# Turning h earlier among the transposes of a fused attention and mixture-of-experts kernel

## The chip, the core and the metric

The kernel runs as one program on one core of a Trainium2 chip. The metric is the device time of one execution in microseconds (us). Three executions of the kernel before took 520.6, 523.1 and 522.89 us, so its median is 522.89 us. The execution that the profiler recorded is a separate one; it took 523.23 us.

A core has five engines with an instruction queue each, and each queue runs in order. TensorE (PE in the profile) multiplies matrices and transposes; PEld is its loading of stationary operands, which overlaps the multiplications. VectorE is DVE, ScalarE is ACT, GpSimd is POOL, SyncE is SP and mostly issues DMA transfers. Engines wait for each other through semaphores.

## The reference

Sigmoid attention over 8 batches, 12 heads, 448 positions and 64 dimensions gives 3584 rows (tokens) of 768 values. Each row that passes a skip test then goes through one of eight experts, and the expert's result, weighted by a gate, is added to the row:

```python
scores = scale * np.matmul(q, k.transpose(0, 1, 3, 2)) - np.log(S)
attn = 1.0 / (1.0 + np.exp(-scores))
x = np.matmul(attn, v)            # then as rows of 12 * 64 = 768 values
do_compute = (x @ w_skip) > 0
xc = x[do_compute]
logits = xc @ w_gate
e_idx = np.argmax(logits, axis=1)
# gate_w: the softmax weight of the chosen expert
for e in range(8):
    mask = e_idx == e
    h = np.maximum(xc[mask] @ w1[e], 0.0)           # 768 -> 1024
    y[mask] = gate_w[mask, None] * (h @ w2[e])      # 1024 -> 768
out = x.copy()
out[do_compute] = xc + y
```

The change touches only the expert part: `xc @ w1`, the ReLU, and `h @ w2`.

## The kernel before, in words

**Attention** comes first, in 48 steps of two heads each, until about 285 us of the profiled span. It also sorts the tokens by expert into a list in DRAM. Two blocks of 128 tokens of the fullest expert follow, written out one by one (`b0`, `b1`), until about 324 us.

**The loop.** The other tokens go through a loop of 14 rounds, from 324.6 us to the end. Each round takes one block of tokens of one expert and branches on its kind:

- a full block of 128 tokens, `block(i, last)`. Its weights are there as two parts, `wh` (rounded to the type fp32r) and `wl` (what the rounding left), and so is its input, `xh` and `xl`. A product is the sum of three: high by high, high by low, low by high. With `last` true the block also splits the raw weights of the next expert (`hi1`, `hi2` on ScalarE, `lo1`, `lo2` on VectorE).
- a 64-token block, `half(i)`, in plain fp32 from the raw weights.
- a 32-token block, `few(i)`, likewise in plain fp32.

In this run the order of kinds is: full, half, full, half, then full and few in turn five times. That makes seven full blocks, two half blocks and five few blocks. The first and the sixth full block are those with `last` true.

**Order of the work.** The body of each kind stands in a manual schedule: every engine runs its instructions in the order in which the code issues them, and the framework adds only the semaphores. What is written earlier is queued earlier on its engine.

**A full block.** `gemm1(h, ...)` makes one half (512 columns) of h with 18 matmuls of 512 columns into the PSUM bank `ph[h]`. `relu(h)` on ScalarE moves it to `hs` in SBUF. `turn_h(h)` transposes it with four transposes of 128x128 into `pht[h]`. `split_h(h)` makes `hh[h]` on ScalarE and `hl[h]` on VectorE. `gemm2(j)` (six matmuls of 384 columns) uses one of eight 128-column pieces of h: pieces 0 to 3 come from the first half, 4 to 7 from the second. In between, the rows of the next block, `xn`, are transposed by `turn_x` (three transposes for each of two halves, into `pxt`); `fetch` then lets GpSimd gather the rows of the block after that into `xn`; `ready_x` copies `pxt` to `xh` and `xf` on ScalarE and subtracts to `xl` on VectorE. At the end `weigh_sum` scales the result on VectorE, and `put` adds it to the output by an indirect DMA on GpSimd. In a plain full block `put` holds a `drain` of GpSimd before it looks at the result.

**A half block.** `side` makes h with 24 matmuls, two of which share the PE array: the two halves of h lie on partitions 0 to 63 and 64 to 127 of one bank, `ph[0]`. The ReLU goes to `hs`, four transposes of h go to `pht[0]` (pieces 0 and 1) and `ph[1]` (pieces 2 and 3), ScalarE copies them to `ht`, and 32 matmuls make the result in `py[1]`. `take_rec`, two small copies, is VectorE's first work of the block.

**What stands in the queues around the change.** In the half block VectorE runs, in order: `take_rec`, the two subtractions of `ready_x`, the two scalings of `weigh_sum` and the copies of `advance`. A `last` block ends with these lines, which put five subtractions of 128x768 on VectorE behind all else of that block:

```python
        put(P, last)
        advance(1 if last else 2)
        if last:
            for j in range(3, NK2):
                lo2(j)
```

Of the kernel before, what the change touches and what calls it, by code (L numbers as in the profile page):

```python
# [14 lines left out]
AF = mybir.ActivationFunctionType  # L15
ALU = mybir.AluOpType
# [3 lines left out]
P = 128  # L20
# [3 lines left out]
def kernel(  # L24
# [11 lines left out]
    nc = tc.nc  # L36
# [13 lines left out]
    NK2 = FF // P  # L50
# [23 lines left out]
    ident = const.tile([P, P], F32, name="ident")  # L74
# [52 lines left out]
    def new_s(name):  # L127

        turn[0] ^= 1
        return ps_s.tile([P, 2, 512], F32, tag=f"s{turn[0]}", name=name)  # L130
# [90 lines left out]
    def new_t(name):  # L221

        if ps_t is None:
            return new_s(name)[:, 0, :]
        return ps_t.tile([P, 512], F32, tag="t", name=name)
# [257 lines left out]
        nc.gpsimd.tensor_tensor(lo, r, hi, op=ALU.subtract)  # L483


    def turn_x(x, h, px):
        for j in range(3):
            i = 3 * h + j
            nc.tensor.transpose(  # L489
                px[:, j * P : (j + 1) * P], x[:, i * P : (i + 1) * P], ident  # L490
            )
# [13 lines left out]
    def gemm1(h, part, xh, xl, ph, lag=False):  # L505

        kinds = ((xh, wh1), (xh, wl1), (xl, wh1))
        t = [(2 * j + 3 * (n == 2) if lag else 2 * n * NK1, n, j) for n in range(3) for j in range(NK1)]
        t.sort()
        for n in part:  # L510
            _, kind, j = t[n]
            a, w = kinds[kind]
            nc.tensor.matmul(  # L513
                ph[h],
                a[:, j * P : (j + 1) * P],
                w[j][h],
                start=(n == 0),
                stop=(n == len(t) - 1),
            )

    def relu(h, hs, ph):
        nc.scalar.activation(hs[:, h * H1 : (h + 1) * H1], ph[h], AF.Relu)  # L522

    def turn_h(h, hs, pt):
        for j in range(4):
            m = 4 * h + j
            nc.tensor.transpose(  # L527
                pt[:, j * P : (j + 1) * P], hs[:, m * P : (m + 1) * P], ident
            )

    def split_h(h, pt, hh, hl):
        nc.scalar.activation(hh[h], pt, AF.Copy)  # L532
        nc.vector.tensor_tensor(hl[h], pt, hh[h], op=ALU.subtract)  # L533

    def gemm2(j, hh, hl, py):
        h, m = divmod(j, 4)
        js = slice(m * P, (m + 1) * P)
        parts = [(n, o) for n in range(3) for o in range(2)]
        for n, o in parts:
            a, w = ((hh, wh2), (hh, wl2), (hl, wh2))[n]  # L540
            last = nc.tensor.matmul(  # L541
                half_y(py, o),
                a[h][:, js],
                w[j][:, o * H2 : (o + 1) * H2],
                start=(j == 0 and n == 0),
                stop=(j == NK2 - 1 and n == 2),
            )
        return last

    def half_y(py, o):  # L550
        return py[o][:, :H2] if isinstance(py, list) else py[:, o, :H2]
# [247 lines left out]
    def new_ph(j):  # L799
        one = new_s(f"b{j}_ph")  # L800
        return [one[:, 0, :], ps_b.tile([P, 512], F32, tag="b", name=f"b{j}_ph1")]
# [29 lines left out]
    for h in range(2):  # L831
        px = new_t(f"b0_px{h}")
# [5 lines left out]
    ph = new_ph(0)  # L838
    py = new_s("b0_py")
# [9 lines left out]
    xn = rows_pool.tile([P, DM], F32, name="xn")  # L849
# [4 lines left out]
    ht = rows_pool.tile([P, 4 * P], F32, name="ht")  # L854
    hs = rows_pool.tile([P, FF], F32, name="hs")
# [195 lines left out]
    ph = new_ph(1)  # L1051
# [66 lines left out]
    py = new_s("b1_py")  # L1118
# [6 lines left out]
    pxt = [pxt2[:, h, :] for h in range(2)]  # L1125
# [37 lines left out]
    hh, hl = [], []  # L1163
# [22 lines left out]
    ph = [new_t(f"ph{h}") for h in range(2)]  # L1186
    py = [new_t("py0"), ps_b.tile([P, 512], F32, tag="b", name="py1")]
    pht2 = new_s("pht")
    pht = [pht2[:, h, :] for h in range(2)]
# [22 lines left out]
    def hi1(i, h):  # L1212
        nc.scalar.activation(wh1[i][h], raw1[i][h], AF.Copy)

    def lo1(i, h):
        nc.vector.tensor_tensor(wl1[i][h], raw1[i][h], wh1[i][h], op=ALU.subtract)
# [14 lines left out]
    def look_ahead(col):  # L1231
        for reg, (j, most) in zip(
            (kind_sp, *names), ((TYP, SPLIT), (NXT, NE - 1), (HAS, 1))
        ):
            nc.reg_mov(reg[ET.SP], entry(j, col, SP, most))
# [79 lines left out]
    def take_rec():  # L1315

        nc.vector.tensor_copy(recs[:, 2, 0:2], rn[:, 0:2])
        nc.vector.tensor_copy(rid[:, 0:1], recs[:, 0, 1:2])
# [4 lines left out]
    def block(i, last):  # L1323


        def split1(js, h):
            if last:
                for j in js:
                    hi1(j, h)
                for j in js:  # L1330
                    lo1(j, h)

        look_ahead(ds(i + 3, 1))
        gemm1(0, range(G1), xh, xl, ph, last)
        relu(0, hs, ph)
        split1(range(3), 0)
        gemm1(1, range(9), xh, xl, ph, last)
        turn_h(0, hs, pht[0])
        split_h(0, pht[0], hh, hl)
        take_rec()  # L1340
        split1(range(3, NK1), 0)
        gemm1(1, range(9, G1), xh, xl, ph, last)
        relu(1, hs, ph)
        for h in range(2):
            turn_x(xn, h, pxt[h])
        fetch()
        split1(range(3), 1)
        gemm2(0, hh, hl, py)
        turn_h(1, hs, pht[1])
        split_h(1, pht[1], hh, hl)  # L1350
        split1(range(3, NK1), 1)
        if last:
            for h in range(2):
                whole_x(h, (slice(0, 3),))
        else:
            ready_x()
        next_rec(i)
        for j in range(1, NK2):
            gemm2(j, hh, hl, py)
        if last:  # L1360
            for j in range(2):
                hi2(j)
            for h in range(2):
                hi_x(h, pxt[h], xh)
            for j in range(2, NK2 - 2):
                hi2(j)
            for j in range(3):
                lo2(j)
            for j in range(NK2 - 2, NK2):
                dve.tensor_copy(wh2[j], raw2[j])  # L1370
            for h in range(2):
                lo_x(h, pxt[h], xh, xl)
        for o in range(2):
            rows = ys if last else yt
            weigh_sum(rows[:, o * H2 : (o + 1) * H2], half_y(py, o), recs[:, 0, 0:1])
# [5 lines that stand above are left out]
# [70 lines left out]
    def half(i):  # L1451

        nx = named()
        take_rec()

        def side(dst, g, n, a, w, j, most):
            nc.tensor.matmul(  # L1457
                dst[g * MD : (g + 1) * MD, :n],
                a,
                w,  # L1460
                start=(j == 0),
                stop=(j == most - 1),
                tile_position=(0, g * MD),
            )

        for j in range(NK1):
            for h in range(2):
                side(ph[0], h, H1, xf[:, j, :], raw1[j][h], j, NK1)
        turned = (pht[0], ph[1])
        parts = [slice(0, 2 * P), slice(2 * P, 4 * P)]  # L1470
        for s in (slice(0, P), slice(P, 2 * P), parts[1]):
            nc.scalar.activation(hs[:, s], ph[0][:, s], AF.Relu)
        for h in range(2):
            for g in range(2):
                load_w1(g, h, nx)
        for h in range(2):
            turn_x(xn, h, pxt[h])
        fetch()
        for c in range(4):
            nc.tensor.transpose(  # L1480
                turned[c // 2][:, (c % 2) * P : (c % 2 + 1) * P],
                hs[:, c * P : (c + 1) * P],
                ident,
            )
        for s, p in zip(parts, turned):
            nc.scalar.activation(ht[:, s], p[:, : 2 * P], AF.Copy)
        ready_x()

        ht8 = ht.rearrange("p (c h t) -> p c h t", c=4, h=2)
        for n in range(NK2):  # L1490
            c, h = divmod(n, 2)
            m = h * (NK2 // 2) + c
            for o in range(2):
                side(
                    py[1],
                    o,
                    H2,
                    ht8[:, c, h, :],
                    raw2[m][:, o * H2 : (o + 1) * H2],
                    n,  # L1500
                    NK2,
                )
        for g in range(3):
            load_w2(g, nx)
        look_ahead(ds(i + 3, 1))
        for o in range(2):
            s = slice(o * H2, (o + 1) * H2)
            weigh_sum(ys[:MD, s], py[1][o * MD : (o + 1) * MD, :H2], recs[:MD, 0, 0:1])
        next_rec(i)
        put(MD)  # L1510
        advance()
# [58 lines left out]
```

## Time and profile before

| | |
|---|---|
| median of three executions | 522.89 us (520.6 to 523.1) |
| profiled execution | 523.23 us |
| its span, first to last instruction | 521.5 us |
| busy: PE / DVE / ACT / POOL | 506.7 / 292.4 / 278.8 / 239.5 us |
| mean granted TensorE clock | 0.994 |
| first half block, in the span | 343.06 to 355.28 us |
| second half block | 373.70 to 385.93 us |
| last full block | 485.83 to 504.22 us |

The span is 1.73 us shorter than the execution's own time; what lies around it is start and end. A row of the timeline gives the start in us from the span's start, the duration in us from the first start to the last end of its instructions, the engine, the line of the kernel, the operation, out<-in, the shapes, and the count; in brackets stands how long the engine was idle before it, and what ended that. A row of a stretch gives, for each engine, busy us and the number of instructions; then the granted clock, the DMA share and GB/s. A source row gives minimum, median and maximum duration in ns. A matmul's duration holds its latency, so the rate is read from starts, not from durations.

### The profile page before, as it was taken

How to read it: one execution, taken by the hardware profiler on the slowest of the kernel's cores; microseconds unless marked ns; L12 is line 12 of the kernel's file. 1: busy time of each engine (PE TensorE's matmuls, PEld its weight loads, DVE VectorE, ACT ScalarE, POOL GpSimd, SP SyncE). 2: the span in 40 equal slices, each digit the busy share in tenths (PEclk: the TensorE clock that was granted, in tenths of full speed). 3: DMA queues.
4: the chain of work that ended last, by engine and by line, in shares of the span. 5: the costliest groups of instructions: out<-in, count | busy, mean ns of one | idle time of the engine just before them, and what ended most of it. 6: DMA issues, size and time to landing. Idle time of an engine off the chain costs nothing.

```text
span 521.5 us, 15403 instructions
## 1 busy us (share of the span) xinstructions
PE 506.7 (97%) x5031; PEld 343.2 (66%) x5032; DVE 292.4 (56%) x692; ACT 278.8 (53%) x481; POOL 239.5 (46%) x355
## 2 busy tenths in 40 slices
PE   8999999999999999999999999999999999999991
PEld 6885554555555555555445889857769797979790
DVE  3545766667668677776684872582221322349522
ACT  4776786766767866677666212661122323258321
POOL 3523454353556767665775401332331334444534
PEclk9999999999999999999999999999999999999997
DMA  8999977897999999999975105949395878797943
GB/s 206 201 233 194 198 159 153 178 178 171 197 195 239 216 194 205 215 193 224 199 158 111 26 31 163 386 131 356 116 339 214 251 300 283 269 328 234 346 185 47
DMA packets 142081, 107.22 MB, mean 206 GB/s; under 512 B 99163, under 2 KB 114523, under 8 KB 142032
## 3 DMA queue, kind: packets, MB, share of 16 engines
q1 hardware_dynamic: 133792, 96.11, 71.1%
q0 software_dynamic: 4032, 8.51, 6.8%
q10 hardware_dynamic: 4208, 1.95, 1.5%
q8 instruction: 30, 0.49, 0.4%
q14 instruction: 19, 0.16, 0.1%
HBM read 98.49 MB, written 17.56 MB: 223 GB/s over the span
## 4 chain that ended last, share of the span: by engine, by line
PE 91%; DMA 2%; DVE 2%; ACT 1%; issue 1%; POOL 1%; SPq 1%; ACTq 0%; POOLq 0%; DVEq 0%
PE s L209 24%; PE pa L237 23%; PE ph L513 11%; PE py L541 11%; PE b_ph L513 3%; PE b_py L541 3%; PE ph L1388 2%; PE py L1388 2%; PE py L1457 2%; PE ph L1457 2%; PE pxt L489 2%; PE pl L277 1%; PE pht L527 1%; DMA out_dram<-ys,rp 1%; PE pg L294 1%
## 5 line engine op out<-in xcount | busy, mean ns | idle before, releaser
L229 ACT ACTIVATE at<-s,bias 128x896 f32<-128x896 f32 (+1 forms) x191 | 173.5, 914 | 83.0 <-PE s L209 72.3
L209 PE MATMUL s<-x 64*64 64x448 f32 (+1 forms) x1528 | 172.3, 497 | 2.1 <-DVE sel L404 0.8
L237 PE MATMUL pa<-at,v 64*64 64x448 f32 (+1 forms) x1536 | 170.3, 489 | 0.0
L173 POOL COPY kq<-kq 32x896 f32<-32x896 f32 (+1 forms) x96 | 87.5, 912 | 97.6 <-DMA kq<-in_q_dram 48.7
L209 PEld LDWEIGHTS s<-x 64*64 64x64 f32 x1528 | 84.7, 191 | 51.2 <-issue 27.0
L237 PEld LDWEIGHTS pa<-at,v 64*64 64x64 f32 x1536 | 68.3, 133 | 54.1 <-issue 45.6
L191 DVE STREAM_TRANSPOSE x<-kq 128x448 f32<-128x448 f32 x94 | 80.7, 933 | 5.3 <-POOL kq L173 5.3
L247 DVE TENSOR_TENSOR xt<-xt,pa 128x448 f32<-128x448 f32 x48 | 29.8, 620 | 53.0 <-ACT xt L668 53.0
L411 POOL DMA_INDIRECT lst<-rec,idx x32 | 31.8, 995 | 16.7 <-issue 5.3
L483 POOL TENSOR_TENSOR wl<-wr,wh 128x384 fp32r<-128x384 f32 (+1 forms) x28 | 31.2, 1127 | 11.4 <-DVE wh L482 6.9
L252 DVE STREAM_TRANSPOSE y<-xt 128x448 f32<-128x448 f32 x48 | 31.0, 645 | 8.9 <-DMA out_dram<-y 7.4
L533 DVE TENSOR_TENSOR hl<-pht,hh 128x512 fp32r<-128x512 f32 x14 | 9.7, 690 | 41.8 <-ACT hh L532 35.1
L522 ACT ACTIVATE hs<-ph 128x512 f32<-128x512 f32 x14 | 8.4, 599 | 42.1 <-PE ph L513 26.2
L571 POOL DMA_INDIRECT out_dram<-ys,rp x15 | 22.8, 1520 | 16.2 <-POOLq L1537 8.4
L541 PE MATMUL py<-wh,hh 128*128 128x384 f32 x112 | 29.8, 347 | 0.0
L541 PE MATMUL py<-wh,hl 128*128 128x384 f32 x112 | 28.8, 338 | 0.0
L541 PE MATMUL py<-wl,hh 128*128 128x384 f32 x112 | 28.7, 337 | 0.0
L499 DVE TENSOR_TENSOR xl<-pxt,xh 128x384 fp32r<-128x384 f32 x30 | 15.3, 552 | 20.9 <-ACT xf L1087 20.2
L513 PE MATMUL ph<-wl,xh 128*128 128x512 f32 x84 | 26.3, 400 | 0.0
L668 ACT ACTIVATE xt<-pa 128x448 f32<-128x448 f32 x48 | 25.7, 536 | 0.8 <-PE pa L237 0.8
L513 PE MATMUL ph<-wh,xh 128*128 128x512 f32 x84 | 25.4, 399 | 0.0
L513 PE MATMUL ph<-wh,xl 128*128 128x512 f32 x84 | 24.1, 391 | 0.0
(263 smaller groups left out, 650.7 us busy)
## 6 DMA issues: line engine op xcount, KB each, us to landing
raw<-in_moe_w_dram SPq DMA_DIRECT2D x48, 768.0 KB
v<-in_v_dram SPq DMA_DIRECT2D x48, 256.0 KB
out_dram<-y SPq DMA_DIRECT2D x192, 56.0 KB
raw<-in_moe_w_dram SPq DMA_DIRECT2D x7, 1536.0 KB
kq<-in_k_dram SPq DMA_DIRECT2D x46, 224.0 KB
kq<-in_q_dram SPq DMA_DIRECT2D x46, 224.0 KB
wr<-in_moe_w_dram SPq DMA_DIRECT2D x12, 256.0 KB
wr<-in_moe_w_dram SPq DMA_DIRECT2D x16, 192.0 KB
```

The source lines that it names most:

```text
L173: nc.gpsimd.tensor_copy(a[BT:, :, :, :BT], a[:BT, :, :, BT:])
L191: nc.vector.transpose(xs[:, n].rearrange("p (r j) -> p j r", j=NJ), t.rearrange("p (j d) -> p j d", d=D)[:, :, :BT],)
L209: nc.tensor.matmul(sc[m * D : (m + 1) * D, j, : qs.stop - qs.start], xs[r, 0, first::NR7], xs[r, 1, qs], start=True, stop=True,)
L229: nc.scalar.activation(at[:, :, :n], sc[:, :, :n], AF.Sigmoid, bias=bias, scale=SCALE)
L237: nc.tensor.matmul(pa[j * D : (j + 1) * D, r, qs], vt[rs, j, r + c if c < 3 else 3 * (1 - r), :], at[rs, j, : qs.stop - qs.start], start=( ...
L247: nc.vector.tensor_tensor(x, x, pa[:, 1, :S], op=ALU.add)
L252: nc.vector.transpose(y, xts[b][:, hp, :])
L411: put = nc.gpsimd.indirect_dma_start(out=lst[:, :], out_offset=bass.IndirectOffsetOnAxis(ap=idx[:, c : c + 1], axis=0), in_=rec[:, c, :], ...
L483: nc.gpsimd.tensor_tensor(lo, r, hi, op=ALU.subtract)
L513: nc.tensor.matmul(ph[h], a[:, j * P : (j + 1) * P], w[j][h], start=(n == 0), stop=(n == len(t) - 1),)
L541: last = nc.tensor.matmul(half_y(py, o), a[h][:, js], w[j][:, o * H2 : (o + 1) * H2], start=(j == 0 and n == 0), stop=(j == NK2 - 1 and n ...
L668: nc.scalar.activation(xts[b][:, hp, :], pa[:, 0, :S], AF.Copy)
```

## The change

In a full block, the second half of h is turned after two `gemm2` pieces and not after one, and the six transposes of the next rows follow directly on those four of h; before, the six stood ahead of the first `gemm2` piece. `fetch` moves along with them, and the splitting of three weight tiles in a `last` block (`split1(range(3), 1)`) is written ahead of both. In a half block, the second of the three ReLU pieces (128 of 512 columns) moves from ScalarE to VectorE; the first two transposes of h stand after five of the six transposes of the next rows, and the last of those six goes between them and the other two of h; `ht` is copied in four pieces of 128 columns and not in two of 256.

```diff
-    def turn_x(x, h, px):
-        for j in range(3):
+    def turn_x(x, h, px, js=range(3)):
+        for j in js:
             i = 3 * h + j
             nc.tensor.transpose(
                 px[:, j * P : (j + 1) * P], x[:, i * P : (i + 1) * P], ident
@@ block
         gemm1(1, range(9, G1), xh, xl, ph, last)
         relu(1, hs, ph)
+        split1(range(3), 1)
+        for j in range(2):
+            gemm2(j, hh, hl, py)
+        turn_h(1, hs, pht[1])
         for h in range(2):
             turn_x(xn, h, pxt[h])
         fetch()
-        split1(range(3), 1)
-        gemm2(0, hh, hl, py)
-        turn_h(1, hs, pht[1])
         split_h(1, pht[1], hh, hl)
         split1(range(3, NK1), 1)
@@
         next_rec(i)
-        for j in range(1, NK2):
+        for j in range(2, NK2):
             gemm2(j, hh, hl, py)
@@ half
         turned = (pht[0], ph[1])
-        parts = [slice(0, 2 * P), slice(2 * P, 4 * P)]
-        for s in (slice(0, P), slice(P, 2 * P), parts[1]):
-            nc.scalar.activation(hs[:, s], ph[0][:, s], AF.Relu)
+        parts = [slice(c * P, (c + 1) * P) for c in range(4)]
+        nc.scalar.activation(hs[:, parts[0]], ph[0][:, parts[0]], AF.Relu)
+        nc.vector.tensor_scalar(hs[:, parts[1]], ph[0][:, parts[1]], 0.0, None, op0=ALU.max)
+        nc.scalar.activation(hs[:, 2 * P : 4 * P], ph[0][:, 2 * P : 4 * P], AF.Relu)
         for h in range(2):
             for g in range(2):
                 load_w1(g, h, nx)
-        for h in range(2):
-            turn_x(xn, h, pxt[h])
+
+        def turned_h(cs):
+            for c in cs:
+                nc.tensor.transpose(turned[c // 2][:, parts[c % 2]], hs[:, parts[c]], ident)
+
+        turn_x(xn, 0, pxt[0])
+        turn_x(xn, 1, pxt[1], range(2))
+        turned_h(range(2))
+        turn_x(xn, 1, pxt[1], range(2, 3))
         fetch()
-        for c in range(4):
-            nc.tensor.transpose(
-                turned[c // 2][:, (c % 2) * P : (c % 2 + 1) * P],
-                hs[:, c * P : (c + 1) * P],
-                ident,
-            )
-        for s, p in zip(parts, turned):
-            nc.scalar.activation(ht[:, s], p[:, : 2 * P], AF.Copy)
+        turned_h(range(2, 4))
+        for c, s in enumerate(parts):
+            nc.scalar.activation(ht[:, s], turned[c // 2][:, parts[c % 2]], AF.Copy)
         ready_x()
```

## The prediction

> **What bounds the kernel now.** I read the page first, its busy times and the chain that ended last:
>
> ```profile
> PE 506.7 (97%) x5031; PEld 343.2 (66%) x5032; DVE 292.4 (56%) x692; ACT 278.8 (53%) x481; POOL 239.5 (46%) x355
> PE 91%; DMA 2%; DVE 2%; ACT 1%; issue 1%; POOL 1%; SPq 1%; ACTq 0%; POOLq 0%; DVEq 0%
> ```
>
> TensorE sets the end. A change counts by what it adds to or takes from TensorE's own sequence, or from the few us behind the last matmul. Next come the stretches of the first half block, of the sixth full block (which splits weights) and of the last full block: length, then busy us and count of PE, PEld, DVE, ACT, POOL.
>
> ```profile
> 343.06:355.28 12.22, 12.11 (x67) 5.37 (x66) 9.14 (x18) 4.55 (x16) 5.20 (x7) 1.00 0.67 167
> ...
> 460.79:479.20 18.41, 18.41 (x102) 16.53 (x99) 14.07 (x27) 14.75 (x28) 9.61 (x16) 1.00 0.94 317
> ...
> 485.83:504.22 18.39, 18.39 (x102) 16.52 (x99) 6.06 (x17) 5.01 (x14) 7.27 (x18) 1.00 0.90 304
> ```
>
> In full blocks TensorE never idles (18.41 of 18.41): no wait is there to be removed. The half block idles 0.11 us and hides a little more under the latencies of its transposes. VectorE is busy 9.14 of 12.22 us in that half block, much for a block that gives it so little. So I looked at its turn, queue by queue: PE, ACT, DVE.
>
> ```profile
> 347.83 0.60 PE L1457 MATMUL ph<-raw,xf 128*64 128x512 f32 x2
> 348.36 0.87 PE L489 MATMUL pxt<-ident,xn 128*128 128x128 f32 x6
> 349.07 0.38 PE L1480 MATMUL pht<-ident,hs 128*128 128x128 f32 x2
> 349.45 0.41 PE L1480 MATMUL ph<-ident,hs 128*128 128x128 f32 x2
> 349.97 0.54 PE L1457 MATMUL py<-raw,ht 128*64 128x384 f32 x2
> ...
> 348.58 0.72 ACT L1472 ACTIVATE hs<-ph 128x128 f32<-128x128 f32 x3 [3.92 <-PE ph L1457]
> 349.49 0.38 ACT L1486 ACTIVATE ht<-pht 128x256 f32<-128x256 f32 x1 [0.18 <-PE pht L1480]
> ...
> 346.64 4.43 DVE L1224 TENSOR_TENSOR wl<-raw,wh 128x768 fp32r<-128x768 f32 x5
> 350.99 0.16 DVE L1317 COPY recs<-rn 128x2 f32<-128x2 f32 x1
> 351.06 0.15 DVE L1318 CAST rid<-recs 128x1 int32<-128x1 f32 x1
> ```
>
> This is the finding of the whole reading. From 346.64 to 351.07 VectorE still runs the five weight subtractions that the full block before left behind. The half block's own `take_rec` (L1317, L1318) comes after them. The ReLU of this block starts at 348.58, in the midst of them.
>
> **The change part by part.** *First half block.* The new ReLU piece on VectorE is written behind `take_rec`, so it starts at 351.06 + 0.15 = 351.21, whatever ScalarE does. Its price is not in the trace. The nearest rows are the cast of one column, 0.15 us (above), and the scaling of 384 columns out of PSUM; beside it stands the ReLU on ScalarE, 128 columns the shortest:
>
> ```profile
> L1321 DVE TENSOR_SCALAR yt<-py,recs x10: 608/614/618, 373.7 to 504.8; 128x384 f32<-128x384 f32 x10
> ...
> L1472 ACT ACTIVATE hs<-ph x6: 271/278/391, 348.6 to 379.6; 128x128 f32<-128x128 f32 x4, 128x256 f32<-128x256 f32 x2
> ```
>
> So it lies between 0.15 and 0.61 us. A straight line from 2 columns (0.16) to 384 (0.61) gives 0.31 at 128, which I take: ready at 351.52. From a ReLU's end to the transpose that reads it, the trace shows 349.45 - (348.58 + 0.72) = 0.15 us. The second transpose of h starts at 351.67 and not at 349.07 + 0.11 = 349.18. Behind it, in TensorE's order, stand one transpose of the next rows and two of h. At rate a transpose takes 0.11 us (two of h take 0.38 from start to end, one alone lasts 0.27), so the last one starts at 352.00, and the first matmul on `ht` about 0.07 later, 352.07 (its piece of `ht` was ready long before). Before it was 349.97. **The first half block loses 2.10 us**, 1.94 to 2.40 by the bounds of the price. Late next is everything behind: `fetch`, `ready_x`, the result. TensorE finds no idle time afterwards to take it back (18.39 of 18.39 in the last full block), so the end moves as much.
>
> *Second half block.* The full block before it leaves no subtractions, and VectorE is idle:
>
> ```profile
> 379.00 0.88 PE L489 MATMUL pxt<-ident,xn 128*128 128x128 f32 x6
> ...
> 380.62 1.19 PE L1457 MATMUL py<-raw,ht 128*64 128x384 f32 x6
> ...
> 379.23 0.72 ACT L1472 ACTIVATE hs<-ph 128x128 f32<-128x128 f32 x3 [10.62 <-PE ph L1457]
> ...
> 382.54 1.02 DVE L499 TENSOR_TENSOR xl<-pxt,xh 128x384 fp32r<-128x384 f32 x2 [4.86 <-ACT xf L1087]
> ```
>
> The last row says idle from 377.68 on. Here the piece starts with ScalarE's, 379.23, and is ready at 379.54. ScalarE's first piece ends at 379.23 + 0.28 = 379.51, so h's first transpose starts at 379.66, in place of the sixth of the rows. The others follow at 0.11: 379.77, 379.88 (rows), 379.99, 380.10. ScalarE's third piece, now its second, ends near 379.80 and is in time. The first transpose's result is there at 379.66 + 0.27, and the first quarter of `ht` takes 0.28 where the half took 0.38: 379.93 + 0.04 + 0.28 = 380.25. From the copy's end to the matmul were 349.97 - 349.87 = 0.10 us, so 380.35 against 380.62: **gain 0.27 us**, bounds 0 (another quarter late) and 0.40 (all waits of ten transposes gone). Had VectorE's piece 0.61 us, the last transposes would slip to 380.32, still in time.
>
> *Seven full blocks* (56 transposes of h, eight each):
>
> ```profile
> 494.61 0.82 PE L489 MATMUL pxt<-ident,xn 128*128 128x128 f32 x6
> 495.19 0.60 PE L541 MATMUL py<-wh,hh 128*128 128x384 f32 x2
> ...
> 496.32 0.60 PE L527 MATMUL pht<-ident,hs 128*128 128x128 f32 x4
> 496.68 0.59 PE L541 MATMUL py<-wh,hh 128*128 128x384 f32 x2
> 497.11 0.51 PE L541 MATMUL py<-wl,hh 128*128 128x384 f32 x2
> ...
> 494.89 0.60 ACT L522 ACTIVATE hs<-ph 128x512 f32<-128x512 f32 x1 [1.57 <-PE pxt L489]
> 497.10 0.60 ACT L532 ACTIVATE hh<-pht 128x512 fp32r<-128x512 f32 x1 [1.60 <-PE py L541]
> ...
> 493.45 0.69 DVE L533 TENSOR_TENSOR hl<-pht,hh 128x512 fp32r<-128x512 f32 x1 [4.23 <-ACT hh L532]
> ...
> L527 PE MATMUL pht<-ident,hs x56: 270/272/273, 330.9 to 496.6; 128*128 128x128 f32 x56
> ```
>
> A group of six takes 495.19 - 494.61 = 0.58, a group of four 0.36, so one transpose 0.11. The pair of matmuls behind a group takes 0.43 (496.68 to 497.11) where a pair takes 0.35 at rate. The fixed part of a group is 0.36 + 0.08 - 4 x 0.11 = 0.00, with 0.02 for rounding. Joining two groups is worth 0 to 0.02 us a block; I take 0.007, **0.05 us for seven**, at most 0.14.
>
> What is moved here stays covered. The first `gemm2` starts 0.58 earlier, at 494.61, and needs `hl[0]` two pairs later, 495.31; it is ready at 494.14. The transposes of h start at 494.61 + 12 x 0.175 = 496.71 and need the ReLU, ready at 495.49. `hh[1]` starts 0.39 later, 497.49, ends 498.09, and `hl[1]` 0.1 and 0.69 later, 498.9; the ten transposes and two more pieces put their first reader at 499.9 and 500.6. If a cover were gone, TensorE would wait one for one, seven times. In the sixth full block ScalarE is the busier one (14.75 of 18.41 us); the 0.39 there shifts its weight copies and VectorE's tail by as much, which the few block and the next `gemm1` cover. The instructions of `split1` keep their places on ScalarE and VectorE.
>
> *`fetch`*, four small GpSimd operations and a gather, waits for the rows' transposes:
>
> ```profile
> 507.14 0.82 PE L489 MATMUL pxt<-ident,xn 128*128 128x128 f32 x6
> ...
> 496.03 0.24 POOL L1269 TENSOR_TENSOR xn<-xn,zf 128x1 f32<-128x1 f32 x1
> 497.68 1.06 POOL L561 DMA_INDIRECT xn<-out_dram,rp  x1 [0.73 <-PE py L541]
> ...
> 505.45 0.20 POOL L1289 TENSOR_TENSOR jk<-yt 128x2 f32<-128x2 f32 x1 [4.24 <-DVE sv L1311]
> ```
>
> The rows' first transpose ends at 496.71 + 0.44 + 0.27 = 497.42, so `fetch` starts about 1.45 us later than 496.03, and the gather at 499.13. This gather and all gathers of that line landed after:
>
> ```profile
> DMA to landing us min/median/max: 5.2/5.2/5.2
> ...
> DMA to landing us min/median/max: 3.9/5.4/6.8
> ...
> L1286 POOLq DRAIN x5: 2308/2695/4437, 367.5 to 501.0; - x5
> ```
>
> It lands at 504.3, and its transposes come at 507.14: covered by 2.8. What is queued behind it on GpSimd is the drain of `put`. The last one starts at 501.0 and ends 2.31 later, 503.3, that is 0.4 after the landing at 497.68 + 5.2 = 502.9; so I read it as waiting for the gather. It would end at 504.75, and the look at the result comes at 505.45: cover 0.7, in the last block as in the others.
>
> *Sum:* 2.10 - 0.27 - 0.05 = +1.78 us. The profiled execution took 523.23 (span 521.5 and 1.73 around it); it would take 525.0. The median of the runs is 0.34 lower, so I predict 522.89 + 1.78 = **524.7 us**, +0.34%.
>
> **The rivals.** *VectorE is free in both half blocks* (the five subtractions end earlier, or the piece gets ahead of them). For it: the second half block is so. Against it: they run without a gap to 351.07, and the order is fixed. Both would gain: -2 x 0.27 - 0.05 = -0.6, 522.3 us.
>
> *The late gather* ends on the slower side. In the last full block the gather holds the drain, the drain holds the scatter, and behind the scatter stands the last few block's. It decides once the landing takes more than 5.2 + 0.7 = 5.9 us. At the 6.8 of the longest it costs 0.9 more: 525.6, and 525.9 with the dear end of the ReLU's price. For it: the cover shrinks from 2.1 to 0.7 us. Against it: little DMA traffic is left there.
>
> *The clock drops.* After the stall the 5.31 us of matmuls on `ht` (349.97 to 355.28) could run slower. The columns are PE busy, clock, DMA share, GB/s, behind the last matmul of the kernel:
>
> ```profile
> 511.00:512.00 1.00, 0.00 (x0) 1.00 0.99 190
> ...
> 514.00:515.00 1.00, 0.00 (x0) 1.00 0.02 7
> 515.00:516.00 1.00, 0.00 (x0) 0.66 0.00 0
> ```
>
> The clock stays whole for 4.0 us without a matmul; the stall has 2.1 us of idle time, and 352.07 - 348.43 = 3.6 us with the transposes. Were all 5.31 us at half speed, as an upper end, the time would be 524.7 + 5.3 = 530.0 us. The Trainium skill (TensorE: Matmul & The Clock Gate, Part 1 and Part 4, PE-mode transpose) says the clock halves after an idle window of about 3.4 us, and that transposes do not count as busy in the same way. By that rule 3.6 us could be enough, and its window of half speed would cost an estimated 1.7 us, 526.4; by the row it is not.
>
> **How the numbers follow.** Forecast 0.62, own range 524.3 to 525.2 (stall 1.94 to 2.40, gains 0.54 to 0). Free VectorE 0.14, late gather 0.13, clock 0.05; 0.06 is left for scatter, as three executions here lie between 520.6 and 523.1. About 0.5%, 2.6 us, is what a measurement of this kernel can tell from no change: slower begins at 525.5, faster below 520.3. The forecast lies inside, but near enough that 0.06 of its 0.62 falls beyond 525.5 by scatter. With it the late gather (0.12) and the clock (0.05) make slower 0.23; faster has 0.05 by scatter alone; the rest, 0.72, is no change. The range goes from the free VectorE, 522.2, to past the late gather, 526.3, and leaves out the clock and the scatter.
>
> **What would show it.** In the profile after: a ReLU on DVE at about 351.2 in the first half block, behind five L1224; TensorE waiting for it some 2 us, the largest wait of the loop; that stretch 14.3 us long, the second half block 12.0, full blocks 18.4 as before; a drain that ends near 504.75 + 1.8. I am wrong if the ReLU on DVE starts with ScalarE's in both half blocks, if full blocks differ by more than 0.1 us, or if the end waits for the drain.

## The result

The changed kernel is slower. Six executions took 528.64 to 529.36 us, median 528.81; the kernel before, beside it, took 520.6 to 524.61 us, median 523.0. The ratio is 1.0123, with a 95% interval of 1.0100 to 1.0147, so the change costs 5.2 to 7.7 us. The prediction was 524.7 us, range 522.2 to 526.3.

The page of the profile after (span 526.1 us, execution 528.73 us), busy times and the chain that ended last:

```profile
PE 507.9 (97%) x5031; PEld 345.6 (66%) x5032; DVE 291.8 (55%) x694; ACT 279.5 (53%) x483; POOL 238.1 (45%) x355
PE 93%; DVE 2%; DMA 2%; POOL 1%; issue 1%; ACT 0%; POOLq 0%; DVEq 0%; ACTq 0%
```

TensorE still sets the end, but its busy time grew by only 1.2 us (506.7 before). Most of the loss is therefore idle time of TensorE. The next view cuts the loop into its stages: each from the first matmul into `ph` to that of the next stage. The columns are length, then busy us and count of PE, PEld, DVE, ACT and POOL, then the granted clock, the DMA share and GB/s. In order: first full, first half, second full, second half; then sixth full, the few block behind it, last full.

```profile
322.44:343.31 20.87, 18.42 (x98) 16.56 (x99) 15.18 (x27) 14.29 (x26) 5.22 (x8) 1.00 0.76 284
343.31:355.78 12.47, 12.40 (x66) 6.24 (x66) 6.33 (x13) 3.06 (x14) 4.17 (x9) 1.00 0.75 233
355.78:374.17 18.39, 18.39 (x100) 16.57 (x98) 4.14 (x12) 3.96 (x12) 3.84 (x9) 1.00 0.66 240
374.17:386.59 12.42, 12.35 (x68) 4.91 (x67) 3.15 (x11) 3.05 (x14) 4.93 (x11) 1.00 0.70 203
461.41:482.32 20.91, 18.46 (x101) 16.59 (x99) 16.34 (x32) 15.32 (x28) 11.24 (x16) 0.99 0.82 279
482.32:490.28 7.96, 7.96 (x136) 6.14 (x137) 5.79 (x12) 2.52 (x12) 3.80 (x7) 0.82 0.64 141
490.28:508.65 18.37, 18.37 (x101) 16.57 (x98) 4.68 (x13) 5.11 (x14) 5.31 (x15) 1.00 0.87 320
```

Before, the same cut gives:

```profile
324.60:343.06 18.46, 18.46 (x100) 16.36 (x99) 12.21 (x21) 12.87 (x24) 4.98 (x8) 1.00 0.88 330
...
479.20:485.83 6.63, 6.63 (x138) 4.72 (x137) 6.49 (x12) 3.16 (x13) 3.19 (x5) 1.00 0.66 213
```

| stage | before, us | after, us | difference |
|---|---|---|---|
| first full block (splits weights) | 18.46 | 20.87 | +2.41 |
| first half block | 12.22 | 12.47 | +0.25 |
| second half block | 12.23 | 12.42 | +0.19 |
| sixth full block (splits weights) | 18.41 | 20.91 | +2.50 |
| the few block behind it | 6.63 | 7.96 | +1.33 |
| the other nine stages together | | | -0.08 |
| loop, first matmul to last | 186.24 | 192.84 | +6.60 |

The loop's 6.60 us lie inside the interval of the runs. The two spans differ by less, 4.6 us, because this execution reached the loop 2.16 us earlier (322.44 against 324.60).

Most of the loss stands in the two *full* blocks that split weights, and not in the half block. The waits of TensorE in the loop (who waits, for whom, us in total, times, longest) say where it goes. Before, this list is empty.

```profile
PE ph L1389 <- DVE ys L1321: 2.5, 1, 2.5
PE ph L1458 <- DVE ys L1321: 2.4, 1, 2.4
```

L1458 is the matmul of a half block, L1389 that of a few block, L1321 VectorE's scaling in `weigh_sum` of the block *before*. The timeline of PE and DVE at the sixth full block's end:

```profile
479.36 0.51 PE L541 MATMUL py<-wh,hl 128*128 128x384 f32 x2
482.32 4.23 PE L1389 MATMUL ph<-raw,xf 128*32 128x128 f32 x96 [2.45 <-DVE ys L1321]
...
479.59 1.02 DVE L1371 CAST wh<-raw 128x768 fp32r<-128x768 f32 x2
480.53 1.01 DVE L499 TENSOR_TENSOR xl<-pxt,xh 128x384 fp32r<-128x384 f32 x2
481.46 1.13 DVE L1321 TENSOR_SCALAR ys<-py,recs 128x384 f32<-128x384 f32 x2
482.51 0.16 DVE L1311 COPY sv<-recs 128x4 f32<-128x4 f32 x1
482.70 0.18 DVE L1313 COPY recs<-sv 128x4 f32<-128x4 f32 x1
```

TensorE ends the block at 479.87 and starts the next one at 482.32. Nothing of the few block needs the scaled result. What it waits for is the first of the two scalings, which starts at 481.46, takes 0.60 and ends at 482.06. VectorE is late because it still had casts of weights and the subtractions of `ready_x` to do.

**The wait that the forecast did not have.** VectorE's ReLU piece reads `ph[0]`. The next round's first matmul into `ph[0]` must not overwrite it before it has been read, so in the changed kernel that matmul waits for VectorE too (in the trace of the kernel before, the first matmuls of a half or few block wait for ScalarE and for DMAs alone). My theory: the loop decides its branches while it runs, so the wait can't name the piece and counts back from the end of VectorE's round. In a half block 8 instructions of VectorE follow the piece (two subtractions, two scalings, four copies of `advance`). So the first matmul of *every* round waits until all but the last 8 of VectorE's instructions of the round before are done, whatever that round was. In a block that splits weights the last 8 are the second scaling, two copies of `advance` and the five subtractions of L1224; the ninth from the end is the first scaling. That is the instruction in the list of waits. In plain rounds the ninth from the end is done long before.

### The profile page after: what moved, and what is told of

It reads as the page before. It is cut to its first block, busy times and chain, and to the rows that moved or that the text cites. A ratio compares the mean times of both kernels' runs of the same rounds, so it can differ in the third digit from the quotient of the medians.

```text
span 526.1 us, 15391 instructions
## 1 busy us (share of the span) xinstructions
PE 507.9 (97%) x5031; PEld 345.6 (66%) x5032; DVE 291.8 (55%) x694; ACT 279.5 (53%) x483; POOL 238.1 (45%) x355
## 4 chain that ended last, share of the span: by engine, by line
PE 93%; DVE 2%; DMA 2%; POOL 1%; issue 1%; ACT 0%; POOLq 0%; DVEq 0%; ACTq 0%
PE s L209 25%; PE pa L237 23%; PE ph L513 11%; PE py L541 11%; PE b_ph L513 3%; PE b_py L541 3%; PE ph L1389 2%; PE py L1389 2%; PE ph L1458 2%; PE py L1458 2%; PE pxt L489 2%; PE pl L277 2%; PE pht L527 1%; DMA out_dram<-ys,rp 1%; PE pg L294 1%
## 5 line engine op out<-in xcount | busy, mean ns | idle before, releaser
L499 DVE TENSOR_TENSOR xl<-pxt,xh 128x384 fp32r<-128x384 f32 x30 | 15.3, 552 | 24.3 <-ACT xf L1087 18.1
```

## The experiments

All ratios are against executions of the kernel before that ran beside each kernel on the same chip. The rival theories were: the forecast's (VectorE's piece stands behind L1224), a loss in the full-block edit, and a wait carried over from round to round.

**E1, the full-block edit alone.** The kernel before with the edit of `block` only:

```diff
+        split1(range(3), 1)
+        for j in range(2):
+            gemm2(j, hh, hl, py)
+        turn_h(1, hs, pht[1])
         for h in range(2):
             turn_x(xn, h, pxt[h])
         fetch()
-        split1(range(3), 1)
-        gemm2(0, hh, hl, py)
-        turn_h(1, hs, pht[1])
```

> The kernel before with the full block's edit alone (two gemm2 pieces, then the second half of h and the next rows in one group); the half block is that of before. Theory W (the ReLU piece on VectorE gives the first matmul of a later block a wait on VectorE): none of the loss is here, the time is that of before within 0.3%, at most 0.1 us less; the first half block 12.2 us, the second 12.2, the few block behind the sixth full block 6.6. Rival F (the new order in the full blocks makes VectorE late at the end of the two blocks that split weights, and the next block's matmuls wait for it): the two stalls of 2.4 us before the half block and before the few block are here too, 5 to 6 us slower.

Measured: 521.98 against 522.31 us, ratio 1.0003 (0.9985 to 1.0020). The first, the sixth and the last full block:

```profile
322.98:341.32 18.34, 18.34 (x98) 16.53 (x98) 12.66 (x22) 13.31 (x25) 5.76 (x8) 1.00 0.88 324
459.02:477.42 18.40, 18.40 (x102) 16.57 (x99) 13.81 (x27) 14.36 (x27) 9.84 (x16) 1.00 0.94 317
484.20:502.62 18.42, 18.42 (x102) 16.58 (x98) 5.87 (x17) 5.12 (x14) 7.29 (x18) 1.00 0.88 300
```

TensorE idles in none of them. The full-block edit costs and brings nothing; its only other mark is 0.16 us more in the few block behind the sixth (6.79).

**E2, the ReLU piece alone.** The kernel before, where only the second 128 columns go to VectorE:

```diff
-        for s in (slice(0, P), slice(P, 2 * P), parts[1]):
-            nc.scalar.activation(hs[:, s], ph[0][:, s], AF.Relu)
+        nc.scalar.activation(hs[:, :P], ph[0][:, :P], AF.Relu)
+        nc.vector.tensor_scalar(hs[:, P : 2 * P], ph[0][:, P : 2 * P], 0.0, None, op0=ALU.max)
+        nc.scalar.activation(hs[:, parts[1]], ph[0][:, parts[1]], AF.Relu)
```

> The kernel before with one ReLU piece of 128 columns of the half block on VectorE, and nothing else changed. Theory W: nearly the whole loss, 5 to 6 us slower: the first matmul of the half block behind the first full block and of the few block behind the sixth wait some 2.4 us for VectorE, and the half blocks take 0.3 to 0.5 us more for pieces that run one after another. Rival F: no stall, within 0.3% of before. The forecast's own theory (VectorE reaches the piece too late in the first half block): that block alone longer, 2.1 us slower.

Measured: 529.94 us, ratio 1.0138 (1.0115 to 1.0162). TensorE's two longest waits:

```profile
PE ph L1457 <- DVE ys L1321: 2.8, 1, 2.8
PE ph L1388 <- DVE ys L1321: 2.3, 1, 2.3
```

One line of code brings both waits and a loss as large as the whole change's: the loop is 192.64 us long, 6.40 more than before, a little over the 5 to 6 expected. The two blocks that end in a wait have 2.73 and 2.37 us of it, the half blocks 0.32 and 0.25, and the few block behind the sixth full block 0.72 (7.35 us). In that few block the clock stays at 1.00, and yet the 96 matmuls into `ph` take 3.54 us to the next transpose, where they took 2.76 before; 0.18 of that is idle time. What slows them is open.

**E3, the changed kernel with the piece back on ScalarE.** All the rest of the change stays:

```diff
-        nc.vector.tensor_scalar(hs[:, parts[1]], ph[0][:, parts[1]], 0.0, None, op0=ALU.max)
+        nc.scalar.activation(hs[:, parts[1]], ph[0][:, parts[1]], AF.Relu)
```

> The changed kernel with that ReLU piece back on ScalarE (three pieces on ScalarE as before); all else of the change is kept. Theory W: no wait for VectorE, the few block behind the sixth full block 6.6 us, both half blocks 11.9 to 12.3 us, the time 0 to 0.7 us below before, not to be told from it. Rival F: 4 to 6 us slower than before, as the changed kernel.

Measured: 522.4 us, ratio 1.0000 (0.9983 to 1.0018). The two half blocks:

```profile
340.81:352.92 12.11, 12.11 (x68) 5.35 (x67) 8.78 (x18) 4.42 (x17) 5.56 (x9) 1.00 0.66 195
371.33:383.44 12.11, 12.11 (x68) 5.35 (x67) 2.86 (x10) 3.18 (x15) 4.95 (x11) 1.00 0.67 196
```

Without VectorE in the ReLU there is no wait left, and the new order of the transposes gains 0.11 to 0.12 us in each half block: some 0.2 us in all, too little to be told from no change. E1 to E3 clear the full-block edit and blame the piece, but they don't yet say *how* it makes TensorE wait.

**E4 and E5, a longer tail of VectorE's round.** If the wait counts back from the end of the round, then instructions put *behind* the piece in the half block must move the wait to an earlier instruction of the block before, although neither the piece nor that block is touched. The changed kernel, with 6 (E4) or 2 (E5) copies of one column at the end of a half block:

```diff
+    pad = mo.tile([P, 1], F32, name="pad")
...
         put(MD)
         advance()
+        for _ in range(6):
+            nc.vector.tensor_copy(pad, zf)
```

> The changed kernel with six more copies of one column on VectorE at the end of the half block (their result is not used). Theory W in its exact form: the wait counts VectorE's instructions back from the end of the round, eight behind the piece as it stands, and 14 here; behind a block that splits weights the last 14 begin before the casts, so the wait is over when TensorE comes, both stalls are gone and the time falls by 5 to 6 us against the changed kernel, to 0.3 to 1 us above before (the half blocks still 12.6 each). If the wait is for the end of VectorE's work on the result in any count, or the stall has another cause: nothing changes, 5 to 6 us slower than before.

> The changed kernel with two further copies of one column on VectorE at the end of the half block (six in the run before). Theory W, that the wait of the first matmul counts back from the end of the round: ten instructions back, so behind a block that splits weights it ends with the first of VectorE's two subtractions for xl, 0.99 us earlier than with eight (482.07 against 481.08 in the changed kernel's profile). The stall before the few block is 1.4 to 1.6 us and not 2.45, that before the first half block shorter by as much; the sum from the first full block to the last matmul some 1.5 to 3 us below the changed kernel's. If six copies helped because of anything else than the count, two copies change nothing in steps of VectorE's instructions.

E5 measured: 527.05 us, ratio 1.0074 (1.0049 to 1.0098). TensorE's two longest waits in its loop:

```profile
PE ph L1459 <- DVE xl L499: 1.5, 1, 1.5
PE ph L1390 <- DVE xl L499: 1.5, 1, 1.5
```

Two instructions more behind the piece, and both waits now end with the 11th instruction from the end, the first subtraction L499, two places earlier than the first scaling. They shrink from 2.45 to 1.47 us each. The value expected from the rows was 2.45 - 0.99 = 1.46 us.

E4 measured: 526.21 us, ratio 1.0062 (1.0039 to 1.0084). With six more, both waits before the blocks are gone (first and sixth full block 18.34 and 18.39 us), and the wait of my prediction takes their place. VectorE in its first half block (the lines of the kernel lie one further down here), and the wait of TensorE:

```profile
345.66 4.43 DVE L1225 TENSOR_TENSOR wl<-raw,wh 128x768 fp32r<-128x768 f32 x5
350.01 0.16 DVE L1318 COPY recs<-rn 128x2 f32<-128x2 f32 x1
350.08 0.15 DVE L1319 CAST rid<-recs 128x1 int32<-128x1 f32 x1
350.15 0.28 DVE L1474 TENSOR_SCALAR hs<-ph 128x128 f32<-128x128 f32 x1
...
PE pht L1482 <- DVE hs L1474: 1.5, 1, 1.5
```

The piece stands behind five subtractions and `take_rec`, as predicted, and the half block takes 13.99 us, 1.77 more than before. The expectation for E4 had left this wait out (half blocks of 12.6 us, 0.3 to 1 us above before in all), so its time was missed while its waits came out. E5's two places for two instructions show the count, and E4 shows where it leads. In both kernels the few block behind the sixth full block took 1.0 us more than before (7.67 and 7.68); in E4 0.82 us of it is a wait of the next block's first matmul for ScalarE. In E5 0.74 us lies between the first transpose and the first matmul on `ht`, 0.16 in the matmuls on `ht` and 0.15 in those into `ph`; the cause is open.

**E6, VectorE reads SBUF instead of the bank.** If it is the *reading of `ph[0]`* that makes the wait, VectorE may do the same ReLU from `hs`. The changed kernel, with a copy more on ScalarE:

```diff
-        nc.vector.tensor_scalar(hs[:, parts[1]], ph[0][:, parts[1]], 0.0, None, op0=ALU.max)
+        nc.scalar.activation(hs[:, parts[1]], ph[0][:, parts[1]], AF.Copy)
+        nc.vector.tensor_scalar(hs[:, parts[1]], hs[:, parts[1]], 0.0, None, op0=ALU.max)
```

> The changed kernel, but ScalarE copies the piece out of PSUM without the ReLU, and VectorE takes the ReLU in place in SBUF: VectorE works in the half block as in the change, but never reads the bank ph[0]. Theory W (the reading of that bank is what brings the wait): no stall before the first half block nor before the few block behind the sixth full block, which takes 6.6 us; left is the wait that was forecast, the piece behind the five subtractions in the first half block, 1.7 to 2.2 us, and some 0.3 in the second; 2 to 3 us slower than before. Rival: any work of VectorE in the half block brings the stalls; then 5 to 7 us slower.

Measured: 525.84 us, ratio 1.0059 (1.0038 to 1.0080). One wait of TensorE is left in the loop:

```profile
PE pht L1482 <- DVE hs L1474: 1.6, 1, 1.6
```

The waits before the two blocks are gone (first and sixth full block 18.44 and 18.42 us), the few block takes 6.77 us, and the first half block takes 13.93, 1.71 more than before. So the bank makes the one wait, and VectorE's queue makes the other. The second half block takes 12.35 us, 0.12 more than before, where some 0.3 was expected: there ScalarE's three pieces start at 379.60, 379.77 and 379.93 without a wait for VectorE, although VectorE still writes its part of `hs`.

**E7 and E8, the clock before the few block.** The 1.33 us of that few block is not idle time. Its 96 matmuls into `ph` took 4.23 us. PE in stretches of 1 us of the changed kernel, at the end of the first full block and then of the sixth; the columns are length, busy us and count, granted clock, DMA share and GB/s:

```profile
341.00:342.00 1.00, 0.00 (x0) 1.00 0.00 0
342.00:343.00 1.00, 0.00 (x0) 1.00 0.00 0
343.00:344.00 1.00, 0.69 (x4) 1.00 0.00 0
...
480.00:481.00 1.00, 0.00 (x0) 1.00 0.00 0
481.00:482.00 1.00, 0.00 (x0) 0.92 0.00 0
482.00:483.00 1.00, 0.68 (x16) 0.50 0.00 0
483.00:484.00 1.00, 1.00 (x25) 0.50 0.00 0
484.00:485.00 1.00, 1.00 (x27) 0.50 0.00 0
485.00:486.00 1.00, 1.00 (x40) 0.87 0.92 66
```

Both idle times are 2.45 us; the clock halves in the second alone. E7 was to fill this idle time with work of no use, 11 matmuls of the identity into a bank that is free there, at the start of every few block:

```diff
         turned = (pht[0], ph[0])
+        for _ in range(11):
+            nc.tensor.matmul(pht[1][:, :P], ident, ident, start=True, stop=True)
```

> The changed kernel with eleven matmuls of 128 columns on the identity at the start of each few block, into a bank that nothing reads before it is written again: they fill TensorE's idle time while it waits there. If the half clock behind that wait comes from the idle time alone, the 96 matmuls of the few block behind the sixth full block run at full rate, 2.8 us and not 4.2, and the granted clock stays at 1.00; the block still starts as late, since the wait for VectorE remains. The other four few blocks get longer by the eleven matmuls, about 2.4 us each. If the half clock has another cause, the 4.2 us stay.

Measured: one execution of 544.04 us, and no answer to the question. The fill matmuls write a bank that VectorE reads too, so they took the wait upon themselves and ran behind the idle time:

```profile
493.17 4.32 PE L1400 MATMUL pht<-ident 128*128 128x128 f32 x22 [2.35 <-DVE ys L1321]
497.42 1.30 PE L1389 MATMUL ph<-raw,xf 128*32 128x128 f32 x40
...
494.00:495.00 1.00, 1.00 (x6) 0.50 0.00 0
```

All the same they show that the clock halved there again, and this time the fill paid for it (4.3 us against 2.4 in the other few blocks), while the 96 matmuls behind it ran at the full clock. Before the first half block of E7 (2.57 us idle) the clock stayed at 1.00.

E8 is the changed kernel once more, unaltered, for a second profile:

> The changed kernel once more, unchanged, for a second profile: both stalls of 2.4 us are there again in theory W. Whether the clock falls behind none, one or both of them is open: in the first profile it fell behind one of two that were equally long (2.45 us), and in the profile with the ReLU piece alone it fell behind neither (2.76 and 2.31 us).

Measured: one execution of 529.18 us. Both idle times are 2.45 us again, and the few block is slow again, at a mean clock of 0.79:

```profile
483.44:491.62 8.18, 8.18 (x136) 6.36 (x136) 5.79 (x12) 2.52 (x12) 3.93 (x8) 0.79 0.58 133
```

Before the first half block the clock stayed whole. The traces hold more on this than the place. Each half-clock stretch in the loop lasted 3.41 us, and in all ten traces every stretch of whole clock that ends in a drop is a whole multiple of 3.41 us long. So each trace can be cut into steps of 3.41 us that end at a drop. PE in such steps of the changed kernel, around both waits, then of E2, around its first wait:

```profile
341.90:345.31 3.41, 2.00 (x10) 1.00 0.00 0
...
478.43:481.84 3.41, 1.44 (x9) 1.00 0.28 96
481.84:485.25 3.41, 2.93 (x56) 0.50 0.05 5
...
343.06:346.47 3.41, 1.46 (x8) 1.00 0.00 0
346.47:349.88 3.41, 3.41 (x20) 1.00 0.46 52
```

In the changed kernel a step ends 1.04 us into the first idle time, and 1.98 us into the second. Wherever the clock fell in the ten traces, TensorE had been busy for 1.44 us or less of the step before (0.97 in E8, 1.06 in E7); where it was busy for 1.46 or more, the clock stayed whole. This fits every drop and every wait on record, but it is read off afterwards: no run was made to test it, and two values so close don't fix a limit.

## Why the prediction was wrong

**The step that failed** is the pricing of the VectorE piece in "First half block": the waits that it brings at the ends of the first and the sixth full block, 2.41 and 2.50 us of the 6.60, stood in the sum at nothing. The step asked what stands *before* the piece in VectorE's queue, and what `ht` needs from it. It did not ask what its *reading of `ph[0]`* asks of the next writer of that bank. I had written that full blocks have no wait to be removed; I did not look for one to be added at their ends. No rival had it either: none adds idle time at the end of a full block. That the forecast said slower was luck, since the loss that it summed, 2.10 us behind L1224, doesn't occur in the changed kernel. The price stood in the trace of before, in the rows of VectorE's scalings at the ends of the two blocks that split weights:

```profile
345.30 1.13 DVE L1321 TENSOR_SCALAR ys<-py,recs 128x384 f32<-128x384 f32 x2
...
480.71 1.14 DVE L1321 TENSOR_SCALAR ys<-py,recs 128x384 f32<-128x384 f32 x2
```

TensorE began the next stages at 343.06 and 479.20. Each row holds two scalings of 0.6 us, so the first ones end at 345.90 and 481.31: 2.84 and 2.11 us after TensorE's start. E2 then measured waits of 2.76 and 2.31.

**First half block, +2.10.** The mechanism is real, though smaller than its bounds of 1.94 to 2.40: E4 and E6, without the earlier wait, lose 1.77 and 1.71 us there. In the changed kernel it doesn't appear, because TensorE has already lost 2.45 us. The subtractions end before h is ready, and the piece starts behind ScalarE's, not behind L1224. DVE and ACT in the first half block after:

```profile
343.79 4.43 DVE L1224 TENSOR_TENSOR wl<-raw,wh 128x768 fp32r<-128x768 f32 x5
...
349.28 0.29 DVE L1473 TENSOR_SCALAR hs<-ph 128x128 f32<-128x128 f32 x1 [0.92 <-ACT hs L1472]
...
348.97 0.28 ACT L1472 ACTIVATE hs<-ph 128x128 f32<-128x128 f32 x1 [7.16 <-PE ph L1458]
349.61 0.38 ACT L1474 ACTIVATE hs<-ph 128x256 f32<-128x256 f32 x1 [0.36 <-DVE hs L1473]
```

So one queue's lateness was paid earlier, and once. The piece's own price was right: taken at 0.31 us, measured at 0.29.

**Second half block, -0.27.** Wrong in sign: +0.19. I had let VectorE's piece start *with* ScalarE's. The rows above show ScalarE, VectorE, ScalarE one behind the other, each waiting for the one before, though the columns differ; in the second half block the starts are likewise 379.78, 380.08 and 380.41. The Trainium skill (PSUM — Partial Sum Buffer, section "PSUM bank collisions raise a hardware error") says that two engines must be kept apart by bank and partition quadrant and not by address, even where both only read; this trace agrees, with ScalarE idle for 0.36 us until VectorE has read. With ScalarE alone (E3) the new order gains 0.12 us, under half of the 0.27.

**Seven full blocks, -0.05.** Right: the five that split no weights took 18.37 to 18.39 us, and E1 gave 1.0003. The covers named for the moved steps held. **`fetch` and the drain:** the late gather did not show. GpSimd's look at the last full block's result ended its idle time on VectorE's copy, not on the drain:

```profile
509.88 0.19 POOL L1289 TENSOR_TENSOR jk<-yt 128x2 f32<-128x2 f32 x1 [4.71 <-DVE sv L1311]
```

The drain had ended at 507.77, so the cover was 2.1 us and not 0.7. That was luck: this gather landed 3.8 us after its issue, where the prediction took 5.2.

**The clock rival** had the right kind of loss at the wrong place: after the wait before the few block, where it cost 1.3 us, and not inside the half block. Where the forecast's own stall came, in E4, the clock stayed whole: its step of 3.41 us (347.48 to 350.89) had TensorE busy for 1.90 us, 1.43 of it with transposes.

**What would show it wrong.** I had named a ReLU on DVE that starts with ScalarE's as a sign against the forecast. It starts directly behind ScalarE's in both half blocks, and the largest wait of the loop is not for it.

**Closing the sum:** two waits 4.91, the few block at half clock 1.33 (its matmuls into `ph` take 1.41 more, its transposes 0.08 less), the half blocks with the chained pieces 0.44, all else -0.08, together 6.60 us. At the whole clock that block can lose time as well, as E2's 0.72 us show.

## What to carry to other kernels

When an operation moves to another engine, list not only what it waits for and who needs its result, but who writes next what it *reads*: that writer gets a wait on the new engine, in this loop at the start of every round and counted back from the end of the round before. Price it where the engine ends its rounds latest, from the rows of the trace of before (here 345.90 against 343.06). A second reader of one PSUM bank brought no parallel work here either, since the pieces ran one after another.

## What the runs showed of the hardware

The clock halved in idle times of 2.45, 2.45 and 2.35 us before the few block (the changed kernel twice, and E7), 1.98, 2.44 and 2.76 us after the last matmul of the full block; in E7 the fill had begun by then. It did not in idle times of 2.45, 2.45 and 2.57 us before the first half block of the same executions, nor in E2's 2.76 and 2.31. The Trainium skill (TensorE: Matmul & The Clock Gate, Part 1) speaks of an idle window of about 3.4 us that runs freely. These traces agree with such steps of 3.41 us, but no whole step had to be idle: the one before the first drop had 1.44 us of busy TensorE and 1.98 us of idle time. So the length of an idle time alone doesn't tell whether the clock falls; where the steps lie in it matters as well. Three drops at one place and none at the other may be chance.
